# One shared product bank for early pairs, the other for weight conversion; later pairs' inverse in PSUM; a constant moved into a logarithm's bias; a new hand-written plan

## The chip, the cores and the metric

The kernel runs on one core of a Trainium2 chip. The engines are TensorE (PE; its weight loads are shown as PEld), VectorE (DVE), ScalarE (ACT), GpSimd (POOL) and SyncE (SP), which here only issues DMA transfers. SBUF is the working memory, PSUM the memory of eight banks that TensorE writes. The metric is the device time of one execution in microseconds (us); the figure compared is the median of several runs.

## The reference

Attention with normalised queries and keys, and then a gated feed-forward block, all in float32:

```
def rmsnorm(x, g):
    rms = np.sqrt(np.mean(x * x, axis=-1, keepdims=True) + 1e-06)
    return x / rms * g
q_n, k_n = (rmsnorm(q, g_q), rmsnorm(k, g_k))
scores = scale * np.matmul(q_n, k_n.transpose(0, 1, 3, 2))
attn = softmax(scores)                      # written out with max, exp and sum
x = (attn @ v), heads joined                # (8*448, 12*64)
out = (silu(x @ w_gate) * (x @ w_val)) @ w_out
```

Batch 8, 12 heads, 448 positions, 64 features a head; the feed-forward block is 768 to 1536 to 768. The three weight matrices arrive as 64-bit floats (each 8 bytes) and are turned into float32 by the kernel itself.

## The kernel before, in words

**Tiling.** Heads are worked in pairs: 6 pairs a batch element, 48 pairs in all (`m` = 0 to 47). Batch elements are joined by two into 4 blocks (`n`) for the feed-forward part. Each feed-forward product is a fast matrix multiplication of 3 by 3 by 2 blocks with 15 products instead of 18: "sides" are sums of blocks of weights or activations, named by the numbers 0 to 14, and `UP_ORDER` and `DOWN_ORDER` say in which order the products run. A block has an up part (4 groups `g` of 15 steps, gate and value at each step: 120 products of four matmuls, L1414) and a down part (15 steps of two halves, 8 matmuls or 4 a group, L1592).

**Stages.** The first 12 pairs (`EARLY`) come ahead of everything; then up 0, then down 0 with pairs 12 to 23 between its products, up 1, down 1 with pairs 24 to 35, and so on; down 3 has no pairs.

**A pair.** Loads of q and k on SP (L746 early, L751 later), squares on ACT (L782), their sums on DVE (L802 early and with L806, which adds the small constant; L808 later, with copies on ACT at L818 and the sum with the constant at L822), then the inverse root: logarithm and exponential on ACT (L696, L697) and one Newton step of three small DVE instructions on 16 or 28 elements (L702, L703, L704, in `improve`). POOL scales q and k with it (L842, L849). They are turned over (TensorE L868 with drains L874 on DVE and L876 on ACT early; DVE L880 later). Scores are L926, exponentials L941. The exponentials' sum over keys runs on TensorE for early pairs (L1033 on all of them) and for later pairs first on POOL and DVE (L946, L952) and then on TensorE. The weighted sum of values is L1002.

**The division.** In `attention`, `total` writes the sums into a bank, `invert` turns them (L1069) into the small tile `rd` and takes reciprocals (L1071), `exchange` copies on ACT (L1084), `spread` lays the inverse out over 448 columns (L1088), and `divide` multiplies the joined result by it (L1097). `copy_sums` (L1091, ACT) and `join` (L1094, DVE) empty the two `at` banks of the weighted sum into `xs`. Early pairs lay the inverse into the same bank as the sums: `banks[m % 2]`, so two pairs take turns; the wait on the last reader is `bank_read[m % 2]`. Later pairs lay it into the SBUF tile `rd`, of which there is one.

**Weight conversion.** `convert` handles 24 pieces of 128 x 1152 words: 16 for the up weights (four for each group `g`), 8 for the down weights. A piece is loaded by five transfers (L1214, L1216), scaled twice on ACT (L1224, L1228), treated by DVE (`shift` L1246, `sign` L1252, `round_part` L1258; each on two halves of 576 columns), summed into sides by 12 POOL instructions (L1277, L1280) and stored to DRAM (L1305). Pieces take turns in places of SBUF: XS (two), GT (three), HS, SPARE, ES and PAIRS. Those in ES, PAIRS and the third GT place wait for the sums of the last early pair (`last_exp`), since exponentials live there. The six pieces of the first list (`by_bank` false) run DVE's steps in SBUF; the others go through a PSUM tile of the `st` ring. `up_load` and the like then fetch stored sides into the two `ws` buffers (L1369); the first load of group `g` needs the stores of pieces 4g to 4g+3.

**What sets the order.** `Order` is a planner in the kernel's own Python: every instruction group is a piece with an engine, an estimated duration, a due time (`when`), a rank (subtracted from the due time as its key), its predecessors, and the ring buffers it takes and uses. `run` lists the pieces by a simulated time; the result is the fixed, in-order queue of each engine. `port=True` says that a piece must not overlap another such piece of DVE or POOL in that simulated time. The due times come from `LEAD`, `PAIR`, `MORE` (extra time that the plan gives up 0), and from the lists `turns`, `starts`, `spans` and `counts` at the end of `fast`, which give the pieces of conversion their places and times.

Of the kernel before, what the change touches and what calls it, by code (L numbers as in the profile page):

```python
# [492 lines left out]
def fast(  # L493
# [77 lines left out]

    order = Order(BUFS, dict(logarithms=load_tables))
    tiles = {}
# [114 lines left out]

    def inverse_root(m, sums, of, when, rank=0.0):


        def estimate():
            ss = of()
            rr = take("rr", m, [P, 2 * NC])[0 : ss.shape[0], 0 : ss.shape[1]]
            tiles["rr", m] = rr
            nc.scalar.activation(rr, ss, AF.Ln, scale=GAIN**-2)  # L696
            nc.scalar.activation(rr, rr, AF.Exp, scale=-0.5)  # L697

        def improve():
            ss, rr = of(), tiles["rr", m]  # L700
            times = nc.vector.scalar_tensor_tensor
            times(ss, rr, GAIN**-2, ss, op0=ALU.mult, op1=ALU.mult)  # L702
            times(ss, ss, -0.5, rr, op0=ALU.mult, op1=ALU.mult)  # L703
            times(rr, ss, 1.5, rr, op0=ALU.add, op1=ALU.mult)  # L704
# [16 lines left out]
    def attention(m):  # L721
# [114 lines left out]
        rr = inverse_root(m, sums, sums_of, ready - 14.0, rank)  # L836

# [119 lines left out]
        for j in (3, 0, 1, 2):  # L957
# [54 lines left out]

        bank = banks[m % 2]

# [29 lines left out]
        for j in range(NJ):  # L1044
# [22 lines left out]
        def invert():  # L1067
            rd, rc = take("rd", m, [P, S]), take("rc", m, [P, 2, Q // C])
            nc.vector.transpose(rd[:, 0:Q], tiles[den])  # L1069
            sums = rd[:, 0:Q].rearrange("p (one c i) -> p one c i", one=1, i=C)[:, :, :, 0]  # L1070
# [25 lines left out]
        def divide():  # L1096
# [13 lines left out]
        done_x[b, c] = add(  # L1110
            "DVE", 0.62, when + 5.0, divide, after=[inv, joined],
            uses=held, port=not early,
        )
        if of_bank:
            bank_read[m % 2] = done_x[b, c]
        if b % 2 and c % 3 == 2:
# [81 lines left out]
    def convert(key, src, sums, to, when, place, by_bank):  # L1198

        rank = 20.0 if by_bank else 30.0  # L1200

# [30 lines left out]

        bank = ("st", ("bits", key))

        def half(k):
            part = ts(k, VALUES // 2)
            if not by_bank:
                return part, bits[:, part]
            bank_of = tiles[bank].rearrange("p b t -> p (b t)")
            return part, bank_of[:, 0 : VALUES // 2].bitcast(U32)  # L1240

        def shift(k):
            if by_bank and k == 0:
                take(*bank, [P, 2, TB])
# [15 lines left out]
        last = one  # L1260
        for k in range(2):
            for x, op in enumerate((shift, sign, round_part)):
                last = add(
                    "DVE", 0.76 if by_bank else 0.45 if x == 0 else 0.85, when, lambda k=k, op=op: op(k),
                    after=[last, two], takes=[bank] if by_bank and not k and not x else [],
                    uses=[bank] if by_bank and (k or x) else [], port=not by_bank,
                )

        blocks = dst.rearrange("p (b f) -> p b f", f=P)
# [410 lines left out]

    nc.gpsimd.memset(many, SCALE)
    nc.gpsimd.memset(halves, 0.0)
    for x in range(2):
# [23 lines left out]
    for n in range(4):  # L1707
# [77 lines left out]
```

## Time and profile before

| | us |
|---|---|
| median of the runs (1477.91 to 1479.96) | 1479.49 |
| the profiled execution's own time | 1477.75 |
| its span | 1476.0 |
| PE busy in the span | 1430.8 (97%) |
| DVE busy | 919.6 (62%) |
| ACT busy | 606.8 (41%) |
| POOL busy | 402.3 (27%) |
| mean granted TensorE clock | 0.991 of full speed |

The span is the time from the first to the last instruction that the profile records; the execution's own time has a little around it. A busy PE isn't at its peak, as matmuls overlap and their ends are modelled; so times of stages are read from starts of matmuls, and lost time from the idle gaps ahead of them. "A <- B" in a list of waits says that A sat idle until B was done, by the last semaphore that came; where B had long been done, it was another.

### The profile page before, as it was taken

To read this page: it belongs to the slowest core of one execution; us is meant where nothing else is said; L and a number is where in the kernel's file an instruction comes from. 1 tells how busy PE (TensorE), PEld (TensorE's weight loads), DVE (VectorE), ACT (ScalarE), POOL (GpSimd) and SP (SyncE) were. 2 spreads that over 40 slices of the span, in tenths; PEclk is the share of its full clock that TensorE was granted. 3 is DMA by queue.
4 is the path that set the end of the run, shared out by engine and by line. 5 is a ranking of instruction groups with operands and counts; after the bars stand their busy time and mean duration, and the time that the engine had idled before them with its cause. 6 is when DMAs were issued, how large, how long until landed. Compare 5 with 4: busy or idle time off the path is not lost.

```text
span 1476.0 us, 19358 instructions
## 1 busy us (share of the span) xinstructions
PE 1430.8 (97%) x6726; PEld 680.8 (46%) x6726; DVE 919.6 (62%) x1484; ACT 606.8 (41%) x1222; POOL 402.3 (27%) x470
## 2 busy tenths in 40 slices
PE   6999899999899999999999999999999999999997
PEld 2444455544344455544444455554444445555553
DVE  4789987777888544357876733356787753432533
ACT  5885444466463221345645222245566322122100
POOL 3554786525543100003444200002344310000000
PEclk8999999999999999999999999999999999999999
DMA  6757999854534532543444442354445452222235
GB/s 191 204 175 235 323 337 306 267 148 97 110 78 95 114 102 71 133 110 90 104 86 105 102 120 71 102 128 90 97 96 109 88 132 79 84 94 73 84 98 108
DMA packets 410415, 193.28 MB, mean 131 GB/s; under 512 B 280004, under 2 KB 390852, under 8 KB 410308
## 3 DMA queue, kind: packets, MB, share of 16 engines
q1 hardware_dynamic: 399040, 190.57, 48.4%
q10 hardware_dynamic: 11140, 1.38, 0.7%
q8 instruction: 55, 0.90, 0.3%
q14 instruction: 52, 0.43, 0.1%
q0 software_dynamic: 128, 0.00, 0.0%
HBM read 157.29 MB, written 34.60 MB: 130 GB/s over the span
## 4 chain that ended last, share of the span: by engine, by line
PE 79%; DVE 4%; POOL 2%; DMA 2%; ACT 2%; issue 1%; SPq 1%; POOLq 0%; DVEq 0%; ACTq 0%
PE mm L1414 23%; PE at L1414 23%; PE mm L1592 22%; PE st L926 5%; PE at L1002 5%; PE st L1033 1%; ACT es L941 1%; DMA out_dram<-spare 1%; DVE xs L1131 1%; DMA ws<-up_sides 1%; DMA ws<-down_sides 0%; DVE sums L952 0%; DVE ss L702 0%; POOL sums L946 0%; DVE spare L1640 0%
## 5 line engine op out<-in xcount | busy, mean ns | idle before, releaser
L1414 PE MATMUL mm<-xs,ws 128*128 128x448 f32 x960 | 402.4, 541 | 6.0 <-DMA ws<-up_sides 5.9
L1414 PE MATMUL at<-xs,ws 128*128 128x448 f32 x960 | 401.0, 540 | 0.0
L1414 PEld LDWEIGHTS mm<-xs,ws 128*128 128x128 f32 x960 | 182.3, 191 | 186.7 <-issue 172.9
L1414 PEld LDWEIGHTS at<-xs,ws 128*128 128x128 f32 x960 | 182.6, 190 | 180.3 <-issue 176.4
L849 POOL TENSOR_TENSOR work<-work,rr 128x448 f32<-128x448 f32 x72 | 72.8, 1031 | 449.2 <-DVE rr L704 356.4
L1592 PE MATMUL mm<-gt,ws 128*128 128x448 f32 x448 | 176.8, 545 | 0.7 <-DVE spare L1356 0.7
L926 PE MATMUL st<-work 64*64 64x448 f32 (+1 forms) x1536 | 155.6, 511 | 21.0 <-ACT es L941 8.1
L1352 DVE TENSOR_TENSOR gt<-gt,mm 128x448 f32<-128x448 f32 x64 | 39.6, 620 | 189.6 <-PE mm L1414 188.9
L1592 PE MATMUL mm<-hs,ws 128*128 128x448 f32 x384 | 151.1, 544 | 0.0
L941 ACT ACTIVATE es<-st 128x896 f32<-128x896 f32 x129 | 114.5, 913 | 81.9 <-PE at L1002 67.6
L946 POOL TENSOR_TENSOR sums<-es 128x896 f32<-128x896 f32 x36 | 76.5, 2126 | 209.7 <-PE st L1033 122.1
L1592 PEld LDWEIGHTS mm<-gt,ws 128*128 128x128 f32 x448 | 83.6, 190 | 84.8 <-issue 82.5
L1488 ACT ACTIVATE st<-gt 128x448 f32<-128x448 f32 x96 | 52.5, 548 | 169.4 <-DVE gt L1356 90.1
L1002 PE MATMUL at<-es,v 64*64 64x448 f32 x1032 | 109.1, 542 | 0.0
L1350 ACT COPY gt<-mm 128x448 f32<-128x448 f32 x80 | 42.5, 531 | 155.3 <-PE mm L1414 155.2
L1592 PEld LDWEIGHTS mm<-hs,ws 128*128 128x128 f32 x384 | 71.3, 190 | 71.7 <-issue 69.9
L926 PEld LDWEIGHTS st<-work 64*64 64x64 f32 x1536 | 49.7, 133 | 99.0 <-issue 38.8
L1350 ACT COPY v<-at 128x448 f32<-128x448 f32 x96 | 51.0, 532 | 78.5 <-PE at L1414 78.3
L946 POOL TENSOR_TENSOR sums<-sums,es 128x896 f32<-128x896 f32 x36 | 76.0, 2110 | 2.8
L1002 PEld LDWEIGHTS at<-es,v 64*64 64x64 f32 x1032 | 39.3, 134 | 57.7 <-issue 55.8
L1352 DVE TENSOR_TENSOR v<-v,at 128x448 f32<-128x448 f32 x64 | 39.7, 620 | 41.3 <-PE at L1414 41.2
L1491 DVE SCALAR_TENSOR_TENSOR gt<-st,v 128x448 f32<-128x448 f32 x96 | 59.6, 622 | 7.5 <-DVE v L1356 0.5
(159 smaller groups left out, 1592.1 us busy)
## 6 DMA issues: line engine op xcount, KB each, us to landing
ws<-up_sides SPq DMA_DIRECT2D x32, 1024.0 KB, 5.6
ws<-down_sides SPq DMA_DIRECT2D x16, 1024.0 KB, 5.7
ws<-down_sides SPq DMA_DIRECT2D x28, 512.0 KB, 4.8
ws<-up_sides SPq DMA_DIRECT2D x16, 768.0 KB, 4.9
out_dram<-spare SPq DMA_DIRECT2D x168, 56.0 KB, 2.1
v<-in_v_dram SPq DMA_DIRECT2D x96, 96.0 KB, 2.4
ws<-up_sides SPq DMA_DIRECT2D x32, 256.0 KB, 6.0
ws<-up_sides SPq DMA_DIRECT2D x16, 512.0 KB, 5.8
```

The costliest lines, as they stand in the source:

```text
L849: nc.gpsimd.tensor_tensor(out=tiles["t", m][:, x], in0=tiles["qk", (m, x)], in1=rr.to_broadcast([P, NC, C]), op=ALU.mult,)
L926: nc.tensor.matmul(st[ds(D * x, D), h, 0:n], tiles["KT", m][rows, ds(P * j + D * of_keys, D)], tiles["QT", m][rows, ds(Q * of_queries, n)] ...
L941: nc.scalar.activation(e, tiles["st", (m, j)][:, :, 0 : S * width(j) // P], AF.Exp)
L946: nc.gpsimd.tensor_tensor(out=to, in0=tiles["e", (m, 0)] if j == 1 else to, in1=e, op=ALU.add)
L1002: nc.tensor.matmul(tiles["at", (m, x)][ds(D * h, D), queries], tiles["v", m][rows, j, h], tiles["e", (m, j)][rows, h], start=j == 0, stop= ...
L1033: nc.tensor.matmul(to[ds(D * h + C * x, C)], halves[:, x] if half else many[:, 0:C], term[:, h, 0:Q] if half else term[:, h, ts(x, Q)], st ...
L1350: nc.scalar.copy(to, ps)
L1352: nc.vector.tensor_tensor(out=to, in0=old, in1=ps, op=ALU.add)
L1414: nc.tensor.matmul(ps(), w[:, which, c, at], xs[:, SLOT[x], c], start=fresh and c == 0, stop=c == NC2 - 1, skip_group_check=True,)
L1488: nc.scalar.activation(take(*act, [P, 2, TB])[:, 0, 0:S], to, AF.Silu)
L1491: nc.vector.scalar_tensor_tensor(to, tiles[act][:, 0, 0:S], 1.0 / SCALE, tiles[ready], op0=ALU.mult, op1=ALU.mult,)
L1592: nc.tensor.matmul(banks[s][:, 0:S], w[:, s, g, at], where[x][:, g], start=fresh and g == 0, stop=g == NG - 1, skip_group_check=True,)
```

## The change

1. **Early pairs' sums and inverse use `banks[0]` alone.** `bank = banks[0]`, and `total` waits for `bank_read[0]`, the division of the pair before.
2. **Early conversions use `banks[1]`.** DVE's three steps of a piece of the first list go through that bank in three thirds of 384 columns (nine instructions), no longer through SBUF in two halves (six). The new ring `bits` has one buffer, and the first up product into that bank waits for the last of them. They no longer carry `port`.
3. **Seven early pieces instead of six**, in the places XS, XS, HS, SPARE, GT 1, GT 0, HS; then nine, and eight for the down weights, with new due times; ranks 0 and 20 instead of 20 and 30.
4. **Later pairs' inverse lies in PSUM**: `spread` writes into the pair's first `at` bank once `copy_sums` has emptied it, and `divide` reads it there. That bank is held until the division; `rd` shrinks to the turned sums and is held by `invert` alone.
5. **The constant moves**: the early pairs' extra DVE instruction (L806) goes; the logarithm takes it as a bias from the tile `little`, filled by one more POOL memset at the start, and the Newton step adds it by one of its operands. The three instructions of `improve` stay three.
6. **Plan numbers**: `improve` and the later pairs' sum with the constant (L822) are marked `port`; POOL's sum is put at 2.15 for 2.08; `LEAD` 10.6 for 10, `PAIR` 8.97 for 9, `MORE` 6.4 for 20.

```
-    order = Order(BUFS, dict(logarithms=load_tables))
+    order = Order(dict(BUFS, bits=1), dict(logarithms=load_tables))
...
-    LEAD, PAIR = 10.0, 9.0
+    LEAD, PAIR = 10.6, 8.97
...
-    MORE = 20.0
+    MORE = 6.4
...
-            nc.scalar.activation(rr, ss, AF.Ln, scale=GAIN**-2)
+            bias = little[0 : ss.shape[0]] if tiny else 0.0
+            nc.scalar.activation(rr, ss, AF.Ln, bias=bias, scale=GAIN**-2)
...
-            times(ss, rr, GAIN**-2, ss, op0=ALU.mult, op1=ALU.mult)
-            times(ss, ss, -0.5, rr, op0=ALU.mult, op1=ALU.mult)
+            times(ss, ss, tiny, rr, op0=ALU.add, op1=ALU.mult)
+            times(ss, ss, -0.5 * GAIN**-2, rr, op0=ALU.mult, op1=ALU.mult)
...
             "DVE", 0.63, when + 1.0, improve, after=[first], uses=[("ss", m), ("rr", m)],
-            rank=rank,
+            rank=rank, port=True,
...
-                nc.vector.tensor_scalar_add(sums, sums, D * 1e-6)
...
-            sums = add("DVE", 0.19, ready - 15.0, both, after=[sums], uses=[("ss", m)])
+            sums = add("DVE", 0.19, ready - 15.0, both, after=[sums], uses=[("ss", m)], port=True)
...
-                        "POOL", 2.08, when + 2.0, more_sums, after=[ex[j], ex[0], *adds[-1:]],
+                        "POOL", 2.15, when + 2.0, more_sums, after=[ex[j], ex[0], *adds[-1:]],
...
-        bank = banks[m % 2]
+        bank = banks[0]
...
-            after=[last, *adds] + ([bank_read[m % 2]] if of_bank else []),
+            after=[last, *adds] + ([bank_read[0]] if of_bank else []),
...
-            rd, rc = take("rd", m, [P, S]), take("rc", m, [P, 2, Q // C])
+            rd, rc = take("rd", m, [P, Q]), take("rc", m, [P, 2, Q // C])
...
-                return tiles["rd", m]
+                return tiles["at", (m, 0)][:, 0:S]
...
-        held = [("rd", m)] if not early else [] if of_bank else [den]
+        held = at[:1] if not early else [] if of_bank else [den]
...
-        inv = add("DVE", 0.64, when + 4.8, spread, after=[inv], uses=[("rc", m)] + held, port=not early)
+        inv = add("DVE", 0.64, when + 4.8, spread, after=[inv, copied], uses=[("rc", m)] + held)
...
-        rank = 20.0 if by_bank else 30.0
+        rank = 0.0 if by_bank else 20.0
...
-        bank = ("st", ("bits", key))
+        bank = ("st", ("bits", key)) if by_bank else ("bits", key)
+        parts = 2 if by_bank else 3
...
-            if not by_bank:
-                return part, bits[:, part]
-            bank_of = tiles[bank].rearrange("p b t -> p (b t)")
-            return part, bank_of[:, 0 : VALUES // 2].bitcast(U32)
+            part = ts(k, VALUES // parts)
+            bank_of = tiles[bank].rearrange("p b t -> p (b t)") if by_bank else banks[1]
+            return part, bank_of[:, 0 : VALUES // parts].bitcast(U32)
...
-    turns = [(*XS, *GT[:2], HS, SPARE), (ES, PAIRS, GT[2], SPARE, HS), (ES, PAIRS, HS, SPARE), (ES, HS)]
-    starts = [LEAD - 4.0, FIRST - 20.0, FIRST + 60.0, FIRST + 110.0]
-    spans = [13.0, 8.0, 9.0, 10.0]
-    counts = [6, 10, 6, 2]
+    turns = [(*XS, HS, SPARE, GT[1], GT[0], HS), (ES, PAIRS, GT[2], SPARE, HS), (ES, HS, PAIRS, SPARE)]
+    starts = [LEAD - 4.0, FIRST - 24.2, FIRST + 78.2]
+    spans = [11.0, 8.2, 9.9]
+    counts = [7, 9, 8]
```

More of the change, by code (lines that the diff above doesn't have):

```diff
@@ L649, in fast @@
     gg = const.tile([P, 1], F32, name="gg")
-    LEAD, PAIR = 10.0, 9.0
+    little = const.tile([P, 1], F32, name="little")
+    LEAD, PAIR = 10.6, 8.97
     FIRST = LEAD + EARLY * PAIR + 6.0
@@ L687, in fast, with inverse_root @@
     SCALE = 2.0**8
-    def inverse_root(m, sums, of, when, rank=0.0):
+    def inverse_root(m, sums, of, when, rank=0.0, tiny=0.0):
         def estimate():
@@ L830, in attention @@
             sums = add("ACT", 0.88, ready - 16.0, swap, after=[sums], uses=[("ss", m)])
-            sums = add("DVE", 0.19, ready - 15.0, both, after=[sums], uses=[("ss", m)])
+            sums = add("DVE", 0.19, ready - 15.0, both, after=[sums], uses=[("ss", m)], port=True)
         def sums_of():
             return tiles["ss", m][0:R, 0, 0 : 4 * NJ] if natural else tiles["ss", m][:, 0]
-        rr = inverse_root(m, sums, sums_of, ready - 14.0, rank)
+        rr = inverse_root(m, sums, sums_of, ready - 14.0, rank, D * 1e-6 * natural)
         def scale(x):
@@ L1067, in invert @@
         def invert():
-            rd, rc = take("rd", m, [P, S]), take("rc", m, [P, 2, Q // C])
-            nc.vector.transpose(rd[:, 0:Q], tiles[den])
-            sums = rd[:, 0:Q].rearrange("p (one c i) -> p one c i", one=1, i=C)[:, :, :, 0]
+            rd, rc = take("rd", m, [P, Q]), take("rc", m, [P, 2, Q // C])
+            nc.vector.transpose(rd, tiles[den])
+            sums = rd.rearrange("p (one c i) -> p one c i", one=1, i=C)[:, :, :, 0]
             nc.vector.reciprocal(rc, sums.to_broadcast([P, 2, Q // C]))
@@ L1106, in attention @@
         )
-        held = [("rd", m)] if not early else [] if of_bank else [den]
+        held = at[:1] if not early else [] if of_bank else [den]
         inv = add("ACT", 0.84, when + 4.5, exchange, after=[inv], uses=[("rc", m)])
-        inv = add("DVE", 0.64, when + 4.8, spread, after=[inv], uses=[("rc", m)] + held, port=not early)
+        inv = add("DVE", 0.64, when + 4.8, spread, after=[inv, copied], uses=[("rc", m)] + held)
         done_x[b, c] = add(
             "DVE", 0.62, when + 5.0, divide, after=[inv, joined],
-            uses=held, port=not early,
+            uses=held,
         )
         if of_bank:
-            bank_read[m % 2] = done_x[b, c]
+            bank_read[0] = done_x[b, c]
         if b % 2 and c % 3 == 2:
@@ L1230, in convert @@
         )
-        bank = ("st", ("bits", key))
+        bank = ("st", ("bits", key)) if by_bank else ("bits", key)
+        parts = 2 if by_bank else 3
         def half(k):
-            part = ts(k, VALUES // 2)
-            if not by_bank:
-                return part, bits[:, part]
-            bank_of = tiles[bank].rearrange("p b t -> p (b t)")
-            return part, bank_of[:, 0 : VALUES // 2].bitcast(U32)
+            part = ts(k, VALUES // parts)
+            bank_of = tiles[bank].rearrange("p b t -> p (b t)") if by_bank else banks[1]
+            return part, bank_of[:, 0 : VALUES // parts].bitcast(U32)
         def shift(k):
-            if by_bank and k == 0:
+            if k == 0 and by_bank:
                 take(*bank, [P, 2, TB])
@@ L1260, in convert @@
         last = one
-        for k in range(2):
+        for k in range(parts):
             for x, op in enumerate((shift, sign, round_part)):
                 last = add(
-                    "DVE", 0.76 if by_bank else 0.45 if x == 0 else 0.85, when, lambda k=k, op=op: op(k),
-                    after=[last, two], takes=[bank] if by_bank and not k and not x else [],
-                    uses=[bank] if by_bank and (k or x) else [], port=not by_bank,
-                )
+                    "DVE", 0.76 if by_bank else 0.53, when, lambda k=k, op=op: op(k),
+                    after=[last, two], takes=[bank] if not k and not x else [],
+                    uses=[bank] if k or x else [],
+                )
+        if not by_bank:
+            bank_read[1] = last
         blocks = dst.rearrange("p (b f) -> p b f", f=P)
@@ L1681, in fast @@
     nc.gpsimd.memset(many, SCALE)
+    nc.gpsimd.memset(little, D * 1e-6 * GAIN**-2)
     nc.gpsimd.memset(halves, 0.0)
@@ L1701, in fast @@
     first = [(up_weights, i) for i in range(4 * NG)] + [(down_weights, i) for i in range(2 * NG)]
-    turns = [(*XS, *GT[:2], HS, SPARE), (ES, PAIRS, GT[2], SPARE, HS), (ES, PAIRS, HS, SPARE), (ES, HS)]
-    starts = [LEAD - 4.0, FIRST - 20.0, FIRST + 60.0, FIRST + 110.0]
-    spans = [13.0, 8.0, 9.0, 10.0]
-    counts = [6, 10, 6, 2]
+    turns = [(*XS, HS, SPARE, GT[1], GT[0], HS), (ES, PAIRS, GT[2], SPARE, HS), (ES, HS, PAIRS, SPARE)]
+    starts = [LEAD - 4.0, FIRST - 24.2, FIRST + 78.2]
+    spans = [11.0, 8.2, 9.9]
+    counts = [7, 9, 8]
     todo = iter(first)
-    for n in range(4):
+    for n in range(3):
         for i in range(counts[n]):
```

## The prediction

> **What bounds the kernel now.** The page gives PE 97% of the span, so only what makes TensorE idle or slow counts. I read first the busy time by stage, cut at the starts of matmuls: early pairs, up 0, down 0, up 1, down 1, up 2, down 2, the rest. Columns: stage and length, then busy time of PE, PEld, DVE, ACT, POOL; granted clock, DMA share, GB/s.
>
> ```profile
> 0.00:131.09 131.09, 112.50 (x1254) 49.90 (x1254) 95.60 (x180) 94.69 (x178) 66.23 (x110) 0.96 0.64 188
> 131.09:322.19 191.10, 185.08 (x500) 92.35 (x497) 155.40 (x242) 91.80 (x133) 112.96 (x219) 0.98 0.88 286
> 322.19:498.88 176.69, 169.75 (x1089) 72.02 (x1088) 142.31 (x217) 90.62 (x214) 76.18 (x46) 0.99 0.47 100
> 498.88:684.71 185.83, 185.34 (x530) 92.48 (x528) 85.99 (x145) 64.17 (x122) 12.34 (x10) 1.00 0.39 102
> 684.71:850.50 165.79, 162.65 (x1062) 73.21 (x1061) 123.30 (x201) 78.89 (x186) 61.29 (x38) 1.00 0.47 99
> ```
>
> Block 0 (191.10 + 176.69 = 367.8) is 16.2 us longer than block 1 (185.83 + 165.79 = 351.6) with the same products and as many pairs. The list of TensorE's waits says where, for the whole span:
>
> ```profile
> PE st L926 <- ACT es L941: 8.1, 14, 3.3
> PE mm L1414 <- DMA ws<-up_sides: 5.9, 1, 5.9
> PE st L926 <- DVE rd L1069: 5.5, 3, 3.0
> ...
> PE st L926 <- DVE work L874: 3.8, 2, 2.0
> ```
>
> The third number is the longest single wait. The 5.9 is in up 0: group 1's first weights land late. SP's queue ahead of that load (start, length):
>
> ```profile
> 157.19 0.33 SPq L1305 DMA_DIRECT2D up_sides<-es  x1
> ...
> 163.71 0.36 SPq L1305 DMA_DIRECT2D up_sides<-work  x1
> ...
> 170.26 0.33 SPq L1305 DMA_DIRECT2D up_sides<-gt  x1
> 170.63 3.03 SPq L1214 DMA_DIRECT2D work<-in_moe_w_gate_dram  x3
> 173.70 0.96 SPq L1216 DMA_DIRECT2D work<-in_moe_w_gate_dram  x2
> 174.75 1.20 SPq L1369 DMA_DIRECT2D ws<-up_sides  x2
> ```
>
> Piece 7 (place PAIRS, tile work) is the last that the group needs; it could not be loaded before the early pairs' last sums, at 131 us, as piece 6 (ES) could not. Its store is at 163.71, the group's load at 174.75, and TensorE goes on at 182.71. The 5.5 is in down 0; DVE and, in the last two lines, POOL around the longest of its three waits (0.81, 1.70, 3.02):
>
> ```profile
> 404.65 1.50 PE L926 MATMUL st<-work 64*64 64x448 f32 x16 [3.02 <-DVE rd L1069]
> ```
> ```profile
> 400.25 1.82 DVE L702 SCALAR_TENSOR_TENSOR ss<-rr,ss 128x28 f32<-128x28 f32 x1 [0.16 <-ACT rr L697]
> 402.11 0.19 DVE L703 SCALAR_TENSOR_TENSOR ss<-ss,rr 128x28 f32<-128x28 f32 x1
> 402.33 1.94 DVE L704 SCALAR_TENSOR_TENSOR rr<-ss,rr 128x28 f32<-128x28 f32 x1
> 404.20 0.40 DVE L1069 STREAM_TRANSPOSE rd<-st 128x224 f32<-128x224 f32 x1
> ```
> ```profile
> 399.36 2.67 POOL L946 TENSOR_TENSOR sums<-es 128x896 f32<-128x896 f32 x1 [6.40 <-ACT v L1350]
> 402.11 2.12 POOL L946 TENSOR_TENSOR sums<-sums,es 128x896 f32<-128x896 f32 x1
> ```
>
> Instructions on 28 elements that take 0.19 us otherwise end with POOL's, at 402.07 and 404.27. The transpose that empties the score bank stands behind them on DVE's in-order queue.
>
> **What the skill says.** SBUF — State Buffer, "Who interferes with whom": DVE and POOL share a port pair as an exclusive lock; a DVE instruction with two SBUF inputs fully blocks against a POOL instruction that reads SBUF, one with at most one SBUF input (outside two-port modes) doesn't. The trace agrees: 1.82 and 1.94 us against 0.19; and the division takes 0.62 with a bank as input, 0.875 in the mean with SBUF's `rd`. TensorE: Matmul & The Clock Gate, "Why this matters for your kernels": idle gaps over about 3 us drop the clock. It agrees: after the 5.9 us gap the next two groups of four ran from 182.71 to 188.07, 5.36 us for 3.01. ScalarE: Activation LUTs, "What ACT_TABLE_LOAD costs": a bias given as a pointer adds 0.093 us to one with immediates. The trace shows the logarithm at 0.221 us but not which form; the bound for 12 of them is 0 to 1.1 us, all on ACT ahead of POOL's scaling, with slack of a pair; I take 0.
>
> **Part by part.**
>
> *Seventh early piece (3).* Group 1 then needs one piece after 131 us, number 7, now in ES. The ES piece before was stored at 157.19. Add 4 us until a store is complete (group 0's: store 99.47, load issued 103.38), up to 5 us if a set of loads stands ahead on SP (164.12 to 168.6 here), and 7.8 us from issue to landing (174.75 to 182.57): 169 to 174. Group 1 is due at 131.1 + 30 x 1.503 = 176.2. So the wait goes, with 2 to 7 us in hand: -5.9, and its clock dip -2.35, together -8.2. Groups 2 and 3 had 9 us or more in hand (last stores at 190.3 and 220.6, their loads at 215.3 and 262.1, held by the buffer) and need no piece later than that. What it collides with is the DMA engines, at 1.0 of their share from 170 to 230; but one piece fewer comes after 131, and 240 to 300 shows 0.67 to 1.06, so I charge nothing. Without that room the last down weights, stored at 300.0 before, would be late for a down 0 that starts near 312; that needs a slip of 7 us.
>
> *DVE's early work (2, 3, 5).* Before: 12 + 12 + 12 instructions of 5.30 + 9.83 + 9.70 us, 4.14 a piece. A third of 384 columns isn't in the trace; between 0.62 (448 columns from a bank) and 0.757 (576) the line gives 0.55. 7 x 9 x 0.55 = 34.7, so +9.9. Gone: L806, 12 in 3.88 us. Blocked time of L702 to L704 early: 12.21 us for 36, against 36 x 0.18 = 6.5; up to -5.7 when planned around POOL. Net 0 to +6 us on DVE's 95.6 of 131, and 2.6 on ACT, 6.5 on POOL. It lies beside TensorE's 8.7 us a pair. It can also help: TensorE's two early waits for the drain L874 (1.99 and 1.83) stand behind six uninterrupted conversion steps (107.9 to 111.8, for one). Bounds -4 to +4; I take 0.
>
> *One bank for sums and inverse (1).* `total` of pair m+1 now waits for `divide` of pair m; behind it on PE's queue stands the next pair's scores. In the trace the divisions ended 0.3 to 2.3 us before the next `total` began for nine of ten pairs (for example 50.14 and 51.55), and 2.5 after it for one (126.07 and 123.62). So 0 to +2.5; I take +1 and set against it 1 us from the waits for L874.
>
> *Port marks and inverse in PSUM (4, 6).* In down 0 the four lines L702, L703, L704, L822 took 8.57 + 3.98 + 7.35 + 6.06 = 26.0 us in 43 instructions; at 0.18 that is 7.7, so 18 us of DVE is blocking, against 4.4 in down 1. Marked, they are laid beside POOL's sums rather than under them. The 36 divisions lose 36 x (0.875 - 0.62) = 9.2 us of DVE, with `spread` +0.03 each. On the path: the waits for L1069, 5.5, and the dip (clock 0.96 over 400 to 440, 1.6 us): 7.1 at most. Against it the `at` bank is held until the division. In down 1 a `total` at 723.03 has its division done at 728.6, the next weighted sum at 731.3: 2.7 us in hand. In down 0 the weighted sum often follows `total` at once (359.13, 359.64) while the division ends at 362.7; so 3 us must be filled with down products there. Bounds -7.1 to +3; I take -5. Downs 1 and 2 idle 3.1 and 2.1 us: -2 to +2, I take -0.3.
>
> *Plan numbers.* No cost of their own. `MORE` 20 to 6.4 only shifts due times by 13.6 us.
>
> Sum: -8.2 + 0 - 5 - 0.3 = -13.5 on the span of 1476.0: 1462.5. The median of the runs lies 3.5 above the span (the profiled execution 1.75, the median 1.74 above that): 1466.0.
>
> **The rivals.**
> A, the forecast, 0.47: both of block 0's losses mostly go; 1461 to 1471.
> B, one of them only, 0.22. For it: new queues, and a plan that was 7 us off at up 0's start (124 planned, 131 measured). If only the weights' wait goes, 1471.3; if only down 0's, 1474.5.
> C, more, 0.11: also the early waits (-4) and downs 1 and 2 (-2): about 1460, to 1456.
> D, no difference, 0.07: the weights' wait moves to group 2, or the DMA engines set up 0's length: 1476.5 to 1482.5.
> E, slower, 0.13: the single early bank. Its ring is `total`, `invert`, `exchange`, `spread`, `divide`: 7.5 us from 42.65 to 50.14, of a pair's 8.7. DVE at 87% and ACT at 88% from 80 to 110 us can stretch it. It decides from 8.7 + 13.5 / 11 = 9.9 us a pair; at 10.2 the early stage costs 16.5 more and the time is 1482.5.
> That the marks change nothing is inside B.
>
> **How the numbers follow.** Faster: A, B, C, 0.80; same 0.07; slower 0.13. 0.2% is 3.0 us, about what these runs can tell from no change. The range, 1457 to 1478, takes in A, B and most of C, with the low end of D; A alone has 1461 to 1471.
>
> **What would show it.** Right: no wait of TensorE for `ws` near 176; up 0 near 183 us; L702 to L704 and L822 near 0.2 us in down 0 and no wait of L926 for L1069; L1097 at 0.62; up 0's first product within 4 us of 131. Wrong: TensorE waiting in the early stage for L1097, at the `at` banks in down 0, or for DMA at group 2 or at down 0's start.

## The result

The changed kernel takes 1463.22 us in the median of its four runs (1461.46 to 1465.35), against 1478.97 for the kernel before in four runs: ratio 0.9896, 95% interval 0.9884 to 0.9909, so 15.8 us shorter. The profiled execution took 1464.89 us, its span is 1463.1 (before 1477.75 and 1476.0). Line numbers move by one or two: the up product is L1416, the down product L1594, scores L927, `total` L1034, `invert` L1070, `join` L1095, `divide` L1098, the Newton step L704 to L706.

First the busy time by stage of the changed kernel, columns as in the prediction: stage and length, then busy time of PE, PEld, DVE, ACT, POOL, then the granted clock, DMA share and GB/s.

```profile
0.00:134.66 134.66, 116.42 (x1255) 53.41 (x1255) 98.80 (x198) 98.46 (x181) 69.98 (x119) 0.96 0.67 199
134.66:320.47 185.81, 183.11 (x501) 92.01 (x497) 154.21 (x235) 86.07 (x128) 110.54 (x211) 0.99 0.85 282
320.47:489.12 168.65, 167.18 (x1092) 72.46 (x1089) 125.39 (x217) 88.94 (x213) 70.97 (x46) 1.00 0.51 105
489.12:674.95 185.83, 185.34 (x530) 92.58 (x528) 82.83 (x145) 63.81 (x122) 11.97 (x10) 1.00 0.39 102
674.95:837.00 162.05, 160.73 (x1057) 72.69 (x1056) 113.84 (x198) 78.95 (x186) 61.31 (x38) 1.00 0.47 101
```

The span's 12.9 us come from four places, with a loss in front:

| stage | before | after | difference |
|---|---|---|---|
| early pairs | 131.09 | 134.66 | +3.6 |
| up 0 | 191.10 | 185.81 | -5.3 |
| down 0 | 176.69 | 168.65 | -8.0 |
| down 1 | 164.26 | 162.05 | -2.2 |
| down 2 | 162.99 | 162.10 | -0.9 |
| ups 1 to 3, down 3 | | | 0.0 |

(Down 1 of the kernel before is given here from 684.71 to 848.97, the first product of up 2. The prediction's table cut it at 850.50, one group of products late; so block 0 was 17.7 us longer than block 1, not 16.2.)

TensorE's waits over the whole span, as waiting instruction <- releaser, then sum, count and longest:

```profile
PE st L927 <- ACT es L942: 6.2, 11, 3.1
...
PE at L1003 <- DVE xs L1095: 3.7, 2, 2.6
PE st L927 <- ACT work L884: 3.2, 2, 2.7
PE st L927 <- DVE work L875: 1.8, 1, 1.8
```

Two of the lines shown of before are gone, the 5.9 us for `ws` and the 5.5 us for `rd`. `join` (L1095) in the early stage has grown from 0.4 to 3.7 us, and the wait for the copy of pair 12's queries (L884), 2.7 us of it at the end of up 0, is new. SP's queue shows why the first went (start, length):

```profile
159.53 0.33 SPq L1307 DMA_DIRECT2D up_sides<-es  x1
...
167.39 0.33 SPq L1307 DMA_DIRECT2D up_sides<-work  x1
168.22 1.52 SPq L1371 DMA_DIRECT2D ws<-up_sides  x2
```

Group 1's load is issued at 168.22 instead of 174.75, 0.8 us after the store from `work` was issued: it no longer needs that piece, as the one in ES is now its last. TensorE's products run through 176 to 185 with a start every 1.50 us; the first of group 1 is the second line here:

```profile
178.35 1.67 PE L1416 MATMUL at<-xs,ws 128*128 128x448 f32 x4
179.86 1.67 PE L1416 MATMUL mm<-xs,ws 128*128 128x448 f32 x4
```

### The profile page after: what moved, and what is told of

The parts are those of the page before. It is cut to its first block, busy times and chain, and to the rows that moved or that the text cites. A ratio compares the mean times of both kernels' runs of the same rounds, so it can differ in the third digit from the quotient of the medians.

```text
span 1463.1 us, 19387 instructions
## 1 busy us (share of the span) xinstructions
PE 1429.7 (98%) x6726; PEld 685.1 (47%) x6726; DVE 881.6 (60%) x1493; ACT 605.4 (41%) x1222; POOL 398.3 (27%) x471
## 4 chain that ended last, share of the span: by engine, by line
PE 90%; DVE 3%; ACT 2%; DMA 2%; issue 1%; SPq 1%; POOL 0%; DVEq 0%; ACTq 0%; POOLq 0%
PE mm L1416 25%; PE at L1416 25%; PE mm L1594 23%; PE st L927 8%; PE at L1003 7%; PE st L1034 1%; ACT es L942 1%; PE mm L1034 1%; DMA out_dram<-spare 1%; DMA work<-in_k_dram 1%; DVE xs L1132 0%; PE st L869 0%; DMA xs<-in_moe_w_gate_dram 0%; DVE spare L1642 0%; DVE mm L1252 0%
## 5 line engine op out<-in xcount | busy, mean ns | idle before, releaser
L1416 PE MATMUL mm<-xs,ws 128*128 128x448 f32 x960 | 400.3, 540 | 0.0
L1416 PE MATMUL at<-xs,ws 128*128 128x448 f32 x960 | 400.2, 539 | 0.0
L1416 PEld LDWEIGHTS at<-xs,ws 128*128 128x128 f32 x960 | 182.3, 190 | 178.9 <-issue 174.7
L1416 PEld LDWEIGHTS mm<-xs,ws 128*128 128x128 f32 x960 | 182.4, 190 | 178.8 <-issue 174.1
L850 POOL TENSOR_TENSOR work<-work,rr 128x448 f32<-128x448 f32 x72 | 67.0, 952 | 468.6 <-DVE rr L706 381.9
L1594 PE MATMUL mm<-gt,ws 128*128 128x448 f32 x448 | 176.1, 544 | 0.0
L927 PE MATMUL st<-work 64*64 64x448 f32 (+1 forms) x1536 | 157.6, 517 | 13.7 <-ACT es L942 6.2
L1594 PE MATMUL mm<-hs,ws 128*128 128x448 f32 x384 | 151.8, 546 | 0.0
L1594 PEld LDWEIGHTS mm<-gt,ws 128*128 128x128 f32 x448 | 83.5, 190 | 83.2 <-issue 81.7
L1594 PEld LDWEIGHTS mm<-hs,ws 128*128 128x128 f32 x384 | 71.5, 191 | 72.9 <-issue 71.8
L927 PEld LDWEIGHTS st<-work 64*64 64x64 f32 x1536 | 51.9, 136 | 86.8 <-issue 40.1
L784 ACT ACTIVATE work<-work 128x448 f32<-128x448 f32 (+1 forms) x96 | 55.2, 587 | 25.8 <-DMA work<-in_q_dram 17.1
```

The lines of the kernel that those rows point to most:

```text
L784: nc.scalar.activation(tiles["t", m][:, x], of, AF.Square)
L850: nc.gpsimd.tensor_tensor(out=tiles["t", m][:, x], in0=tiles["qk", (m, x)], in1=rr.to_broadcast([P, NC, C]), op=ALU.mult,)
L927: nc.tensor.matmul(st[ds(D * x, D), h, 0:n], tiles["KT", m][rows, ds(P * j + D * of_keys, D)], tiles["QT", m][rows, ds(Q * of_queries, n)] ...
L1416: nc.tensor.matmul(ps(), w[:, which, c, at], xs[:, SLOT[x], c], start=fresh and c == 0, stop=c == NC2 - 1, skip_group_check=True,)
L1594: nc.tensor.matmul(banks[s][:, 0:S], w[:, s, g, at], where[x][:, g], start=fresh and g == 0, stop=g == NG - 1, skip_group_check=True,)
```

## The experiments

Three groups of edits can stand behind the gain: the seven early pieces with their product bank, the inverse in PSUM, and the port marks. The runs put them in and take them out. Each ratio is to the kernel before, timed in the same batch; "waits for rd" are TensorE's in down 0, sum and count.

| run | pieces early, where converted | inverse | marks | median us | ratio (95%) | early | up 0 | down 0 | waits for rd |
|---|---|---|---|---|---|---|---|---|---|
| before | 6, SBUF | SBUF | no | 1478.97 | 1 | 131.1 | 191.1 | 176.7 | 5.5, 3 |
| e1 | 6, SBUF | SBUF | yes | 1480.71 | 1.0011 (1.0004 to 1.0018) | 135.6 | 195.7 | 174.3 | 2.5, 1 |
| e2 | 6, SBUF | PSUM | no | 1472.51 | 0.9954 (0.9937 to 0.9971) | 134.1 | 191.0 | 170.8 | 1.1, 1 |
| e3 | 7, SBUF | SBUF | no | 1480.5 | 1.0006 (0.9997 to 1.0015) | 137.1 | 185.9 | 178.9 | 6.0, 3 |
| e4 | 6, bank | PSUM | yes | 1473.38 | 0.9962 (0.9947 to 0.9976) | 132.0 | 195.3 | 170.8 | 1.2, 1 |
| e5 | 6, SBUF | own PSUM tile | no | 1483.58 | 1.0033 (1.0021 to 1.0046) | 133.8 | 191.2 | 180.3 | 6.6, 3 (for rc) |
| e6 | 7, bank | PSUM | no | 1465.55 | 0.9909 (0.9892 to 0.9925) | 135.7 | 184.7 | 168.0 | none |
| e7 | 7, SBUF | PSUM | yes | 1482.42 | 1.0024 (1.0015 to 1.0034) | 143.0 | 192.5 | 171.1 | 2.8, 1 |
| e8 | 7, bank, PAIRS sooner | PSUM | yes | 1467.7 | 0.9931 (0.9914 to 0.9947) | 133.5 | 186.0 | 172.2 | 2.8, 1 |
| e9 | 7, bank | SBUF | yes | 1466.42 | 0.9915 (0.9900 to 0.9930) | 136.5 | 184.7 | 168.3 | none |
| e10 | 7, bank, pair 12 sooner | PSUM | yes | 1466.96 | 0.9923 (0.9910 to 0.9937) | 133.5 | 185.8 | 172.6 | 2.8, 1 |
| e11 | 7, bank | SBUF | no | 1468.11 | 0.9928 (0.9911 to 0.9944) | 132.9 | 184.7 | 170.8 | none |
| e12 | 7, bank | PSUM | later pairs | 1463.99 | 0.9898 (0.9881 to 0.9914) | 132.8 | 184.7 | 168.0 | none |
| after | 7, bank | PSUM | yes | 1463.22 | 0.9896 (0.9884 to 0.9909) | 134.7 | 185.8 | 168.7 | none |

The stage lengths are of one profiled execution each; the last section shows that an early stage can differ by some 3 us, and an up 0 by 1, between executions, so small differences in these two are read from the medians.

### e1: the port marks alone

```
(kernel before)
-            rank=rank,
+            rank=rank, port=True,                      # improve
-            sums = add("DVE", 0.19, ready - 15.0, both, after=[sums], uses=[("ss", m)])
+            sums = add("DVE", 0.19, ready - 15.0, both, after=[sums], uses=[("ss", m)], port=True)
```

> The kernel before with the two port marks only (the Newton step and the later pairs' sum with the constant). If blocked small DVE instructions cause down 0's loss: L702, L703, L704, L822 near 0.2 us each in down 0 (26.0 us before), TensorE's waits for L1069 (5.5) gone, down 0 at 169 to 172 us (176.7 before), time 1471 to 1475. If the late, short-held rd or the inverse in SBUF is the cause: down 0 stays above 174 and the time within 3 us of before. Early stage and up 0 as before in both (131, 191).

Measured: 1480.71 us over 20 runs, not faster. The marked lines L702, L703, L704 and L822 (the four small lines from here on) take 27.1 us in down 0, against 26.0 before: there the marks don't lay them beside POOL's work on the chip. In downs 1 and 2 they do: the four lines take 5.9 us in each, 0.18 to 0.19 us an instruction, against 10.2 before, and the two stages are 2.5 and 0.9 us shorter. Down 0 is only 2.4 us shorter, with one wait for `rd` left of three; the early stage and up 0 are 4.5 and 4.6 us longer. In up 0 a wait of 2.9 us for L1356 has joined the one for `ws` (5.0); why the marks bring that is not shown.

### e2: the inverse in PSUM alone

```
(kernel before)
-            rd, rc = take("rd", m, [P, S]), take("rc", m, [P, 2, Q // C])
+            rd, rc = take("rd", m, [P, Q]), take("rc", m, [P, 2, Q // C])
-                return tiles["rd", m]
+                return tiles["at", (m, 0)][:, 0:S]
...   (spread and divide: held, after and port as in the change)
```

> The kernel before with the later pairs' inverse in the at bank only. Division at 0.62 us in both theories. If blocked small instructions are the cause of down 0's loss: they stay, down 0 at 174 to 178, downs 1 and 2 shorter by 0 to 2 each, time 1474 to 1479. If the inverse's place is the cause: no wait for L1069, down 0 at 169 to 172, time 1471 to 1474. If holding the at bank costs: waits of L1002 for L1097, time above 1480.

Measured: 1472.51 us, 6.5 less. Down 0 loses 5.9 us; the four small lines take 19.5 us there instead of 26.0, and the twelve divisions 7.40 instead of 8.98. So in the kernel before this edit, not the marks, shortens down 0. It also changes the written order there (ten of the twelve sums have down products directly behind them, seven before), and the run doesn't separate the two. The wait for group 1's weights is still there (5.25 us, ending at 184.94).

### e3: the seven pieces and the plan numbers, converted in SBUF

```
(kernel before)
-    LEAD, PAIR = 10.0, 9.0
+    LEAD, PAIR = 10.6, 8.97
-    MORE = 20.0
+    MORE = 6.4
-        rank = 20.0 if by_bank else 30.0
+        rank = 0.0 if by_bank else 20.0
...   (turns, starts, spans, counts as in the change; POOL's sum stays at 2.08)
```

> The kernel before with the new lists, ranks and plan numbers only: seven early pieces, in SBUF in halves, two banks for early pairs. If the seventh early piece is what ends group 1's wait: no wait of TensorE for ws near 176, up 0 at 183 to 187 (191.1 before), down 0 as before (175 to 178). Early stage 132 to 136 if the seventh piece's work on DVE is what lengthens it, 130 to 132 if the single bank does that. Time 1471 to 1476.

Measured: 1480.5 us, the same as before and above the 1471 to 1476 expected. Up 0 falls to 185.9 us and has no wait for `ws`: the seventh early piece is enough for that. But the early stage takes 6 us more, and down 0 keeps its three waits for `rd`.

### e4: the change with six early pieces

```
(changed kernel)
-    turns = [(*XS, HS, SPARE, GT[1], GT[0], HS), ...
-    counts = [7, 9, 8]
+    turns = [(*XS, HS, SPARE, GT[1], GT[0]), ...
+    counts = [6, 10, 8]
```

> The changed kernel with six early pieces and ten behind them (XS, XS, HS, SPARE, GT 1, GT 0; then ES, PAIRS, ...). If the seventh piece on DVE lengthens the early stage: its end back from 134.7 to 130 to 132; and group 1 needs two pieces after that again, so TensorE waits for ws near 176 by 2 to 6 us, plus 1 to 2.5 of lower clock: time 1463 to 1467. If the single bank lengthens the early stage: it stays at 134 to 135 and the time is 1467 to 1471.

Measured: 1473.38 us, 10.2 more than the change and above both expectations, since the waits are longer than the 2 to 6 us put. TensorE's waits in the whole span:

```profile
PE mm L1416 <- DVE st L1252: 7.9, 1, 7.9
...
PE mm L1416 <- DMA ws<-up_sides: 2.5, 1, 2.5
```

The first is group 1's weights again, whatever the last semaphore says: in SP's queue their load is issued at 176.97, behind the store of the piece in `work` at 167.97, and TensorE goes on at 185.20. Up 0 is 9.4 us longer without the seventh piece. The early stage is 2.7 us shorter, which one profiled execution of each can't tell from chance (last section).

### e5: the old inverse, but `rd` not held over the reciprocal

```
(kernel before)
-            rd, rc = take("rd", m, [P, S]), take("rc", m, [P, 2, Q // C])
+            rd = take("rd", m, [P, S]) if early else spread_st[0][:, 1]
...   (the later pairs' sums are turned into a PSUM tile; rd is taken by spread)
```

> The kernel before, where later pairs turn their sums inside the PSUM tile they lie in and take rd only at spread, so invert no longer waits for the division of the pair before; the inverse stays in SBUF, the port marks as before. If the one rd buffer is what makes down 0 late: TensorE's waits for L1069 under 2 us (5.5 before), down 0 at 170 to 173 (176.7 before; 170.8 with the inverse in PSUM), time 1472 to 1476. If the inverse's reads from SBUF or its port marks are: down 0 at 175 to 178, time 1477 to 1481.

Measured: 1483.58 us, above both expectations; the waits only change name, 6.6 us in three places for `rc` (L1072). `invert` begins 2.3, 2.5 and 5.1 us after the end of these three sums, as before. So the single buffer `rd` does not hold it back; what is left is the work ahead of it on VectorE's queue.

### e6: the change without the port marks

```
(changed kernel)
-            rank=rank, port=True,
+            rank=rank,
-            sums = add("DVE", 0.19, ..., uses=[("ss", m)], port=True)
+            sums = add("DVE", 0.19, ..., uses=[("ss", m)])
```

> The changed kernel without the two port marks. If they matter for down 0, as the forecast had it: blocked small instructions there up from 15.6 us to over 24, down 0 from 168.7 to over 171, time 1466 to 1471. If they only reorder (alone they gave a ratio of 1.0011): down 0 within 1.5 us, time 1460 to 1466.

Measured: 1465.55 us, 2.3 more than the change with overlapping intervals; down 0 168.0 us with no wait for `rd`. So the marks aren't needed in down 0. In downs 1 and 2 the four small lines take 13.6 us each without the marks and 5.9 with them, and the stages are 0.7 us longer each.

### e7: the change with the early conversions in SBUF and the early pairs on two banks

```
(changed kernel)
-        bank = banks[0]
+        bank = banks[m % 2]
-        parts = 2 if by_bank else 3
...   (VectorE's early steps in two halves in SBUF and marked port, as before)
```

> The changed kernel with early conversions in SBUF in halves, marked port, and the early pairs' sums on two banks in turn. If the product bank is what lets seven pieces fit beside the early pairs: up 0 starts at 137 to 141 (134.7 with the bank), time 1467 to 1475. If the single bank for early pairs costs: up 0 starts at 130 to 133, time 1459 to 1463.

Measured: 1482.42 us, 19.2 more than the change, slower than the kernel before and above both expectations. The early stage of this kernel:

```profile
0.00:143.03 143.03, 114.72 (x1191) 49.81 (x1191) 92.23 (x177) 96.74 (x179) 64.43 (x110) 0.92 0.61 181
```

64 of the early pairs' matmuls run behind the first up product here (1191 records against 1255), so the two stages are best taken together: 335.5 us against 320.5 in the changed kernel. In the early stage VectorE is less busy than in the changed kernel (92.23 against 98.80 us, with fewer instructions), so its load is not what makes it longer. `join` and the drain cost about the same (3.9 and 2.0 us, against 3.7 and 1.8); more is waited for the exponentials (5.2 against 3.9), the drains on ACT (3.9 against 1.5), POOL's scaling (2.9 against 1.5) and `copy_sums` (2.1 against nothing), and the clock is 0.92 against 0.96. In both runs that convert seven pieces in SBUF, e3 and e7, they don't pay; whether that is SBUF itself, the mark `port` that goes with it or the two banks for early pairs is not separated.

### e8 and e10: pair 12's queries sooner

In the changed kernel TensorE waits at the end of up 0, for L884:

```profile
318.02 2.52 PE L927 MATMUL st<-work 64*64 64x224 f32 x16 [2.70 <-ACT work L884]
```

```
e8:  (..., (ES, HS, PAIRS, SPARE)]  ->  (..., (ES, PAIRS, HS, SPARE)]      # the tile of pair 12 is free sooner
e10: ready = base - span  ->  ready = base - span - 4.0 * (m == EARLY)     # pair 12's due times 4 us sooner
```

> The changed kernel with the last list in the order ES, PAIRS, HS, SPARE instead of ES, HS, PAIRS, SPARE, so the place that pair 12's queries and keys use is free one piece (about 10 us) earlier. If its late load causes TensorE's wait of 2.7 us for L884 at the end of up 0 and the lower clock after it: up 0 at 182 to 184 (185.8), time 1458 to 1461. If pair 12 is late for another reason: up 0 within 1 us of 185.8, time 1462 to 1465.

> The changed kernel with the due times of pair 12 (the first after the early twelve) put 4 us earlier. Theory 1 (the 2.7 us wait of TensorE for pair 12's queries at the end of up 0 comes from its transposes' and copy's place in the queues, due times that are too late): the wait for L884 there is gone, and up 0 takes 183 instead of 185.8 us; 1459 to 1462 us if down 0 stays at 168.7. Rival (the written order of everything after it moves with it, and the first down stage loses what up 0 gains, as when group PAIRS was taken earlier): up 0 falls or not, down 0 rises to 170 to 173 us, 1464 to 1468 us.

Measured: 1467.7 us, above both expectations, and 1466.96 us, as the rival had it; both are longer than the change. The wait is there in both (3.9 and 3.8 us) and the copy starts at 317.3 to 317.4 as before. The loads began at 294.4 in the changed kernel, 287.1 in e8, 293.9 in e10, so their time doesn't set it either. In e10's trace the pair's reduction, small steps, POOL scaling and two transposes (307.27 to 317.24) lie between VectorE's work on the last up products. In the kernel before the copy started at 317.70, and TensorE came to it only at 319.29: the wait was close behind, and taking 5.9 us out of up 0 uncovered it. What would bring the pair forward stays open. Both runs also lost 2.8 us in down 0 to a new wait for `rd`: an order written for another due time can differ everywhere after it.

### e9: the change with the inverse back in SBUF

```
(changed kernel)
-                return tiles["at", (m, 0)][:, 0:S]
+                return tiles["rd", m]
...   (rd, held, spread and divide as before)
```

> The changed kernel with the later pairs' inverse back in the SBUF tile rd (division from SBUF, marked for the shared port), all else as changed. Theory 1 (the inverse in PSUM is what shortens the first down stage and the division, with or without the other edits): down 0 comes back to 174 to 178 us from 168.65, the division of the later down stages to 11.2 us per twelve from 7.4, downs 1 and 2 to 163 to 165 from 162.1; in all 1471 to 1477 us. Rival (the seven pieces and the product bank are what shortens the first down stage too, because group 1's weights and the early stage no longer hold anything back, and the inverse's place is worth what the counts of small instructions say, 1 to 3 us in the whole kernel): 1464 to 1467 us.

Measured: 1466.42 us. My theory fell: down 0 stays at 168.3 us without a wait for `rd`, though the four small lines take 20.7 us there (15.6 in the change) and the divisions 9.7. The rival's 1464 to 1467 holds. Downs 1 and 2 are 1.1 and 0.5 us longer, with twelve divisions of 10.4 and 10.6 us against 7.4.

### e11: the change without the marks and without the inverse in PSUM

```
(changed kernel; e6 and e9 together)
```

> The changed kernel with the inverse in SBUF and without the port marks: of the change only the seven early pieces with VectorE's steps in a product bank (and the logarithm's constant as a pointer) are left. Theory 1 (the first down stage is long because TensorE's scores wait for rd, the sums' transposition that VectorE reaches late; the marks or the inverse in PSUM, either one, take these waits away once seven pieces run early): without both the waits for rd in down 0 come back, 5 to 7 us in two or three places, down 0 takes 175 to 179 us from 168.65, in all 1471 to 1476 us. Rival (the pieces in the bank alone take these waits away, since the order that is laid after them differs): no wait for rd over 1 us, down 0 168 to 170 us, 1464 to 1468 us.

Besides the seven pieces and their bank, the single bank for early pairs, the logarithm's bias and the plan numbers are left, 2.15 for POOL's sum among them. Measured: 1468.11 us, so 11.5 of the 15.8 us come without marks and without the inverse in PSUM. The rival is right again: no wait for `rd`. The blocking by POOL is still there, and `invert` (L1070) is as late as before. VectorE in down 0 of this kernel:

```profile
360.01 2.06 DVE L704 SCALAR_TENSOR_TENSOR ss<-ss,rr 128x28 f32<-128x28 f32 x1
...
362.33 1.95 DVE L706 SCALAR_TENSOR_TENSOR rr<-ss,rr 128x28 f32<-128x28 f32 x1
...
364.74 0.40 DVE L1070 STREAM_TRANSPOSE rd<-st 128x224 f32<-128x224 f32 x1
```

and TensorE at the same time:

```profile
358.63 0.59 PE L1034 MATMUL st<-sums,many 128*32 128x224 f32 x8
359.14 6.28 PE L1594 MATMUL mm<-gt,ws 128*128 128x448 f32 x16
365.36 1.74 PE L927 MATMUL st<-work 64*64 64x448 f32 x16
```

`invert` began 5.5 us after the end of the sums (L1034), as in the prediction's example of before (5.1 us). But here 16 down products of 6.28 us stand between the sums and the next scores on TensorE's queue, and the bank is empty when they are reached. In the kernel before TensorE had this behind its sums:

```profile
398.51 0.58 PE L1033 MATMUL st<-sums,many 128*32 128x224 f32 x8
399.03 0.98 PE L1002 MATMUL at<-es,v 64*64 64x448 f32 x8
399.90 0.98 PE L926 MATMUL st<-work 64*64 64x448 f32 x8
400.70 0.93 PE L1002 MATMUL at<-es,v 64*64 64x448 f32 x8
```

Some 3 us of work, and then the scores that wait 3.02 us for `rd` at 404.65. (The `st` ring has two tiles, so it is the second tile of scores behind a pair's sums that needs the bank of the sums.) The kernel before has the other case too, later in the same down 0:

```profile
467.41 0.59 PE L1033 MATMUL st<-sums,many 128*32 128x224 f32 x8
467.92 3.27 PE L1592 MATMUL mm<-hs,ws 128*128 128x448 f32 x8
471.04 3.17 PE L1592 MATMUL mm<-gt,ws 128*128 128x448 f32 x8
474.87 3.27 PE L1592 MATMUL mm<-gt,ws 128*128 128x448 f32 x8 [0.66 <-DVE spare L1356]
478.07 1.73 PE L926 MATMUL st<-work 64*64 64x448 f32 x16
```
```profile
475.26 0.41 DVE L1069 STREAM_TRANSPOSE rd<-st 128x224 f32<-128x224 f32 x1
```

`invert` is 7.3 us late here, and no scores wait for it. Over all twelve sums of down 0: in the kernel before and in e3 the first five have attention work directly behind them, and three of these waited; the last seven have down products there, and none waited. In e11 eleven of twelve have down products directly behind them, and the twelfth has them behind one group of scores. `invert` was 5.0 and 7.3 us late after two more of its sums (at 380.02 and 393.75), without a wait either. Down products are no guarantee: in e7, e8 and e10 one group of eight stood behind a sum whose `invert` was 6.0 to 6.1 us late, and the scores waited 2.8 us.

### e12: marks on the later pairs alone

```
(changed kernel)
-            rank=rank, port=True,
+            rank=rank, port=m >= EARLY,                # improve
```

> The changed kernel with the marks for the shared port on the later pairs' root steps alone, not on the early twelve's. Theory 1 (the marks matter in the down stages at most; on the early pairs they cost nothing, since nothing but the order of small VectorE instructions moves): the early stage 134 to 136 us, down 0 168 to 169 us, 1461 to 1466 us, the same as the changed kernel. Rival (the marks hold the early pairs' chain back behind POOL's scaling and rounding): the early stage 131 to 133 us, 1458 to 1461 us.

Measured: 1463.99 us, the same as the change. Its profiled early stage is shorter (132.8 us), as the rival had it, but its time is not; so the early pairs' marks cost nothing that these runs can tell.

## Why the prediction was right, and where its steps were not

**The time.** 1466.0 was forecast and 1463.2 measured; rival A. On the span 13.5 us less were worked out, 12.9 came. That is closer than the single terms: early 0 against +3.6, up 0 -8.2 against -5.3, down 0 -5 against -8.0, downs 1 and 2 -0.3 against -3.1. Their errors are 2.8 to 3.6 us each and cancel, which is luck.

**Seventh early piece: right, and shown from both sides.** e3 has it with the plan numbers and no wait for `ws`; e4 takes it out and waits 7.9 and 2.5 us. The load was issued in two parts, at 168.22 and 168.8; the second landed 9.3 us later, at 178.1 (of the first the trace gives no landing). That is 43.4 us after the first up product, where 38 to 43 were forecast, and the need lies 30 x 1.503 = 45.1 us after it, at 179.8. The products never stopped, but the margin is 1.7 us, not 2 to 7. The sum missed 3.9 us of what comes next: 2.70 us for pair 12's queries, and 1.16 us more for the 16 scores behind it (2.52 against the 1.36 they took before). The prediction asked what else the earlier up 0 would meet, but only among the DMA engines and the last down weights; the first scores after the up products were not looked at. Some 1 us of the difference isn't assigned.

**Early work of VectorE and one bank: harmless, as put, but not zero.** A third took 0.55 to 0.56 us (forecast 0.55), and VectorE's early busy time grew by 3.2 us, inside 0 to +6. Rival E was not seen: no wait for a division through the single bank in the changed kernel, and in e4, with the same bank, the early stage takes 132.0 us. The two waits for the drain became one, 2.0 us less, and `join` costs 3.3 us more, behind the conversion's thirds. TensorE's idle time in the stage is the same (18.6 before, 18.2 after); the 3.6 us are in its busy time (112.5 to 116.4 for the same matmuls), that is in slow stretches of this execution. What the step didn't see is the size of what it avoided: with the early pieces back in SBUF and two banks the change takes 19 us longer (e7).

**Port marks and inverse in PSUM: the waits of down 0 went, but not by the step's reason.** Forecast were "laid beside POOL's sums rather than under them" and -5 within -7.1 to +3; -8.0 came, outside these bounds. The 5.5 us of waits are gone, and TensorE's busy time in the stage is 2.6 us less (clock 0.99 to 1.00). The small instructions did not come near 0.2 us there: 15.6 us for 44 of them, 0.35 in the mean. The marks alone leave them where they were (27.1 us, e1), and in the changed kernel neither the marks (e6), nor the inverse (e9), nor both (e11) are needed for the waits to go. VectorE does come sooner in the changed kernel: the latest `invert` of down 0 begins 1.5 us after its sums, 2.9 without the marks, 6.6 without the inverse in PSUM, 7.3 without both, and 7.3 before. (This hangs on the order too: e8 and e10 have both edits, and 6.1 and 6.0 us at one sum.) But whether a late `invert` costs anything depends on what TensorE has to do between a pair's sums and the scores that need their bank: in the changed kernel, e6, e9 and e11 down products stand behind every sum, directly or after one group of scores. Which part of the rest of the change brings this order is not separated. The lists and most plan numbers alone don't (e3 has the order of before); the product bank, the single early bank, the bias and 2.15 for POOL's sum are left.

Taken out of the change, the inverse is worth 3.2 us, the marks 2.3, both 4.9 (e9, e6, e11), of which the first two are near the uncertainty. The sum by parts was wrong in kind: e1, e2 and e3 alone give +1.7, -6.5 and +1.4 us, and no sum of them makes -15.8.

**Bias as a pointer.** L698 takes 0.310 us in the median early, where L696 took 0.216 (the prediction's 0.221). These 0.094 us fit the 0.093 that the Trainium skill states (ScalarE: Activation LUTs, "What ACT_TABLE_LOAD costs"); all twelve together take 3.75 us of ACT instead of 2.59, within the prediction's bound but for 0.1, and TensorE has no new wait for them.

**Downs 1 and 2: here the step's reason held, and it was priced too low.** Put at -0.3 within -2 to +2, measured -3.1, outside these bounds too. The four small lines take 5.9 us in each of the two stages instead of 10.2, and the twelve divisions 7.4 instead of 11.3. Down 1 and down 2 together take 327.3 us before, 327.0 without marks and inverse (e11), 325.8 with the marks alone (e9), 325.5 with the inverse alone (e6) and 324.2 with both. So each is worth about 1.5 us here, and together they make nearly the whole gain. (These are single profiled executions. The six kernels with both edits, e4, e7, e8, e10, e12 and the change, lie between 324.1 and 324.6; of those with neither, before, e5 and e11 lie between 327.0 and 327.3, and e3 at 329.9.)

## What to carry to other kernels

Before an instruction's lateness is priced, look at what its consumer's queue holds in between: a transpose 5.5 us late cost nothing where 16 down products stood in between, one 5.1 us late cost 3.0 where 3 us of attention did. Where a planner writes the order, an edit can be a new order; test it inside the full change and take it out there, since parts that gave +1.7, -6.5 and +1.4 us alone made -15.8 with the rest of the change. And for each wait that an edit removes, list what the freed engine reaches next and when that is ready.

## What the runs showed of the hardware that was not expected

The same gap on TensorE is sometimes followed by a slow stretch and sometimes not. e2 has, in its records, the same order on every engine as the kernel before up to the start of down 0. The kernel before in its early stage:

```profile
93.40 0.98 PE L926 MATMUL st<-work 64*64 64x448 f32 x8 [1.99 <-DVE work L874]
94.20 2.44 PE L1002 MATMUL at<-es,v 64*64 64x448 f32 x24
```

and e2 at the same place:

```profile
94.34 0.99 PE L926 MATMUL st<-work 64*64 64x448 f32 x8 [2.00 <-DVE work L874]
95.14 4.13 PE L1002 MATMUL at<-es,v 64*64 64x448 f32 x24
```

A gap of 1.99 us with no loss, and one of 2.00 us after which 24 matmuls took 1.7 us more, the granted clock being 1.00 and 0.83 from 90 to 100 us (1.00 in both from 85 to 95). The end of up 0 repeats it; e12 beside the line of the changed kernel shown with e8:

```profile
316.19 1.36 PE L927 MATMUL st<-work 64*64 64x224 f32 x16 [2.69 <-ACT work L884]
```

2.69 us of idleness and 1.36 us for the scores, against 2.70 and 2.52, at a granted clock of 1.00 and 0.50 in these scores. e6, e9 and e11 have the gap of 2.69 us and 1.36 us for the scores, too. The prediction leaned on the Trainium skill's gap of about 3 us (TensorE: Matmul & The Clock Gate, "Why this matters for your kernels"); here shorter gaps, of 2.0 and 2.7 us, had a slow stretch behind them in some executions and none in others. So a profiled stage with such gaps can be some 3 us off from one execution to the next (the early stage of before and of e2, 131.1 and 134.1 us, with the same order), and part of the +3.6 us of the changed kernel's early stage may be no more than that.
